# Splitting bn_stats passes over three slots, and a list scheduler that lets VectorE wait for a product

## The chip, the cores and the metric

One core of a Trainium2 chip. The metric is the device time of one execution in microseconds (us), lower is better. The kernel before had a median of 213.98 us in three runs (213.87 to 214.91).

The profiler's span is about 1.7 us shorter than the device time (212.9 us and 214.63 us for the profiled execution of before).

## The reference

```python
x = A_x                                   # (1, 2048, 512) bf16
xn = _layernorm(x)
# A: linear attention with softmax feature maps, 32 heads of 16
q, k, v = split(xn @ wqkv)
phi_q, phi_k = [softmax(+p), softmax(-p)] of q @ w_phi, k @ w_phi
o = (phi_q @ (phi_k^T v)) / (phi_q @ sum(phi_k) + 1e-6)
# B: gated bilinear unit, 1792 wide
h = (xn @ w_gate) * (xn @ w_up)
out = x + o @ wo + h @ w_down
```

## The kernel before

The kernel records steps (engine, function, tiles read and written) and a list scheduler orders them engine by engine. TensorE's order and the DMA queue's are pinned as recorded; those of VectorE, ScalarE and GpSimd follow from modelled costs. `prio` 0 is urgent, 1 normal, 2 filler. The parts that the change and the argument touch:

```python
def features(name, t, w, b=None):         # exponentials of +p and -p, their sums, logarithm, reciprocal
    ...
    dve(lambda e: e.tensor_reduce(out=sm, in_=e_v, axis=AX.X, op=ALU.add), ...)        # L506, "reduction"
    act(ln_v[:, n, :, sel], sm[:, :, sel], [("sums", sr)], [("ln", n)], func=ACTF.Ln)

def ln_apply(t):                           # L454, "normalisation"; xn has four slots
    ...
    dve(lambda e: e.tensor_scalar(out=xn_tile(t), in0=x_tile(t), ...), ..., [("xn", t % 4)] + ...)

def x_turn(t):                             # a transposing DMA from an xn slot: the slot is free when it has landed
    sc.dma(SP, lambda e: e.dma_start_transpose(o, xn_tile(t)), [("xn", t % 4)], [("xnT", t)], ..., turn=True)

def moments(chunks, after):                # sum of squares of the up weights, from bn_stats; L668
    sc.prio = 2
    for i in chunks:
        dve(lambda e, i=i: e.bn_stats(wst[:, i, :], wu_chunks[:, i, :]), keys + after, [("wst", i)], 512)
    ...

def gate(ft, sg, bg, bu, s):               # "product" of gate and up, L894: frees a bank (one of its output buffers) that TensorE needs
    act(g, bank(bg), ...)                  # the gate copy, ScalarE
    sc.prio = 0
    dve(lambda e: e.tensor_tensor(out=h_v[...], in0=bank(bu), in1=g, op=ALU.mult), ...)
    sc.prio = 1

def late_loads(t):
    ...
    elif t == 5:
        load_w(SP, wd_v, B_w_down..., "wd", 1835008)       # 1792 KB, ahead of the next transposes in the queue
        load_w(SP, wo_v, A_wo..., "wo", 524288)

def scales(t):
    ...
    if t in (5, 6):
        moments(range(7 * (t - 5), 7 * (t - 4)), last)

def _order(sc):
    ...
        soon = min(begin(p) for p in lst) + 100.0
        cand = min((p for p in lst if begin(p) <= soon), key=lambda p: (steps[p[1]].prio, begin(p), p[1]))
```

## Time and profile before

| | before, profiled execution |
|---|---|
| device time | 214.63 us (median of three runs 213.98) |
| span | 212.9 us |
| TensorE busy | 208.2 us, 98% |
| VectorE, ScalarE, GpSimd busy | 167.3, 143.8, 109.9 us |
| start of the first gate matmul (the first of 256 columns) | 9.07 us |
| from there to the end | 203.83 us |

Part 1 of the page of before (engine, busy us, share of the span, instructions) and the head of part 4, the chain of work that ended last:

```profile
PE 208.2 (98%) x1455; PEld 125.3 (59%) x1476; DVE 167.3 (79%) x281; ACT 143.8 (68%) x350; POOL 109.9 (52%) x137
...
PE 96%; DMA 1%; DVE 1%; issue 1%
```

TensorE bounds the kernel. How close it is to its limit cannot be judged by its busy share, because matmuls are pipelined, as the Trainium skill says ("Perfetto Trace Analysis", Identifying the Most-Contended Engine). This trace agrees: a matmul of 512 columns is drawn 379 ns long although the next one starts 216 ns after it, so a stall of up to 0.16 us leaves no idle time on TensorE. What shows the stalls is the distance from each matmul's start to the next. In this trace it is 216 ns for 512 columns, which agrees with the 215.7 ns of the skill ("TensorE: Matmul & The Clock Gate", Wait — 56ns, not 53.3ns?). After 10 us there are 21 steps one whole matmul too long. 1455 matmul records stand beside 1476 weight loads, so 21 records are missing; these steps are no stalls. Three others are: 0.133 us at 55.41, 0.143 us at 58.38 and 0.102 us at 60.24, together 0.38 us.

They show as idle times of the weight loads in the timeline of before (start us, us, engine, line, operation, tiles, shapes, count, and in brackets the idle time before and what ended it):

```profile
55.41 0.55 PEld L247 LDWEIGHTS ps<-arena 128*128 128x128 bf16 x4 [0.46 <-DVE arena L894]
...
58.37 0.55 PEld L247 LDWEIGHTS ps<-arena 128*128 128x128 bf16 x4 [0.47 <-DVE arena L894]
...
60.23 0.23 PEld L381 LDWEIGHTS ps<-arena 128*128 128x128 bf16 x4 [0.43 <-ACT arena L228]
```

The timeline of before, VectorE, leads to them (L454 normalisation, L894 product, L668 bn_stats, L506 reduction):

```profile
48.22 0.68 DVE L668 BATCH_NORM_STATS2 arena<-arena 128x6 f32<-128x512 bf16 x1
51.11 0.41 DVE L454 TENSOR_SCALAR arena<-arena 128x512 bf16<-128x512 bf16 x1 [2.20 <-DMA arena<-arena]
51.44 0.68 DVE L894 TENSOR_TENSOR arena<-ps,arena 128x512 bf16<-128x512 f32 x1
52.04 0.41 DVE L454 TENSOR_SCALAR arena<-arena 128x512 bf16<-128x512 bf16 x1
52.36 1.28 DVE L668 BATCH_NORM_STATS2 arena<-arena 128x6 f32<-128x512 bf16 x2
53.55 1.20 DVE L506 TENSOR_REDUCE arena<-arena 128x64 f32<-128x1024 bf16 x1
54.67 0.68 DVE L894 TENSOR_TENSOR arena<-ps,arena 128x512 bf16<-128x512 f32 x1
55.27 2.46 DVE L668 BATCH_NORM_STATS2 arena<-arena 128x6 f32<-128x512 bf16 x4
57.65 0.67 DVE L894 TENSOR_TENSOR arena<-ps,arena 128x512 bf16<-128x512 f32 x1
```

VectorE stands 2.20 us in front of a normalisation whose xn slot a transposing DMA still reads. A ready product, two bn_stats and the reduction queue behind it. ScalarE then waits for the reduction (timeline of before, ScalarE), and its gate copies are late in turn:

```profile
54.79 0.26 ACT L228 ACTIVATE arena<-arena 128x64 f32<-128x64 f32 x1 [3.17 <-DVE arena L506]
```

### The profile page before, as it was taken

The page shows a single profiled execution, that of the slowest core. Times are in us where ns is not written, and L with a number is a line of the kernel's source. Part 1 is how long each engine was busy: PE and PEld are TensorE (multiplying, and loading weights), DVE is VectorE, ACT ScalarE, POOL GpSimd, SP SyncE. Part 2 cuts the span into 40 slices and gives each one's busy share as a digit, 9 for nine tenths or more (in the row PEclk, how much of TensorE's full clock was granted, in tenths as well). Part 3 has the DMA queues.
Part 4 walks back from the last instruction along what each step waited for, and adds up shares of the span by engine and source line. Part 5 has one row for each costly group of instructions (what it writes and reads, how often), then busy time and mean ns, then how long its engine had stood idle before and what let it go on. Part 6 is the DMA issues. An engine that isn't in the chain of part 4 may idle for free.

```text
span 212.9 us, 4028 instructions
## 1 busy us (share of the span) xinstructions
PE 208.2 (98%) x1455; PEld 125.3 (59%) x1476; DVE 167.3 (79%) x281; ACT 143.8 (68%) x350; POOL 109.9 (52%) x137
## 2 busy tenths in 40 slices
PE   8999999999999999999999999999999999999995
PEld 3575444444444444444444444546888898899884
DVE  4687999985995656578699988996888898898622
ACT  5479899975789999987778977664544444432220
POOL 4031554540311355999995882004549559558540
PEclk9999999999999999999999999999999999999999
DMA  5999780899100030322721340413374646537611
GB/s 163 309 300 375 134 207 0 122 345 147 30 3 0 20 78 3 52 51 49 77 45 29 65 86 0 118 53 52 45 83 125 162 85 154 134 91 175 123 49 49
DMA packets 49251, 22.29 MB, mean 105 GB/s; under 512 B 38096, under 2 KB 47696, under 8 KB 49232
## 3 DMA queue, kind: packets, MB, share of 16 engines
q1 hardware_dynamic: 48272, 21.39, 46.0%
q10 hardware_dynamic: 960, 0.66, 1.0%
q8 instruction: 11, 0.18, 0.4%
q14 instruction: 8, 0.07, 0.2%
HBM read 11.03 MB, written 2.10 MB: 62 GB/s over the span
## 4 chain that ended last, share of the span: by engine, by line
PE 96%; DMA 1%; DVE 1%; issue 1%
PE ps L247 91%; PE ps L611 2%; PE ps L553 2%; DMA arena<-in_A_x_dram 1%; PE ps L381 1%; PE ps L474 1%; DVE arena L427 0%; DVE arena L924 0%; DVE arena L434 0%; PE ps L1001 0%
## 5 line engine op out<-in xcount | busy, mean ns | idle before, releaser
L247 PE MATMUL ps<-arena 128*128 128x512 bf16 (+2 forms) x1139 | 198.4, 329 | 1.1
L247 PEld LDWEIGHTS ps<-arena 128*128 128x128 bf16 (+1 forms) x1160 | 110.7, 98 | 73.8 <-ACT arena L228 1.2
L228 ACT ACTIVATE arena<-ps 128x512 bf16<-128x512 f32 (+3 forms) x117 | 58.6, 539 | 12.9 <-PE ps L247 7.0
L228 ACT ACTIVATE arena<-arena 128x32 f32<-128x32 f32 (+9 forms) x131 | 52.9, 423 | 11.3 <-DVE arena L506 7.2
L894 DVE TENSOR_TENSOR arena<-ps,arena 128x512 f16<-128x512 f32 (+1 forms) x56 | 38.2, 683 | 11.8 <-PE ps L247 6.1
L516 POOL TENSOR_TENSOR arena<-arena 128x1024 bf16<-128x1024 bf16 x16 | 31.8, 1995 | 26.8 <-ACT arena L228 26.8
L506 DVE TENSOR_REDUCE arena<-arena 128x64 f32<-128x1024 bf16 x32 | 38.2, 1210 | 7.6 <-ACT arena L228 7.5
L228 ACT ACTIVATE arena<-ps,arena 128x512 bf16<-128x512 f32 (+1 forms) x55 | 35.9, 672 | 10.9 <-PE ps L247 10.4
L855 POOL TENSOR_TENSOR arena<-arena 128x256 f16<-128x256 f16 x32 | 23.8, 755 | 14.3 <-DMA arena<-arena 13.2
L833 DVE TENSOR_TENSOR arena<-arena 128x896 f16<-128x896 f16 x32 | 26.0, 812 | 3.4 <-PE ps L247 3.4
L228 ACT ACTIVATE ps<-ps 128x256 f32<-128x256 f32 x24 | 8.8, 368 | 29.0 <-PE ps L247 27.0
L924 DVE SCALAR_TENSOR_TENSOR arena<-ps,arena 128x256 bf16<-128x256 f32 (+1 forms) x24 | 13.2, 565 | 8.9 <-PE ps L247 8.7
L773 POOL TENSOR_TENSOR arena<-arena 128x512 f16<-128x512 bf16 x14 | 16.3, 1175 | 5.7 <-DVE arena L894 5.2
L959 POOL TENSOR_TENSOR arena<-arena 128x512 f32<-128x512 f32 x8 | 9.5, 1190 | 17.0 <-ACT arena L228 17.0
L522 POOL TENSOR_TENSOR arena<-arena 128x512 bf16<-128x512 bf16 x16 | 17.0, 1060 | 0.8
L621 DVE TENSOR_TENSOR arena<-ps,arena 128x512 f16<-128x512 f32 x16 | 11.0, 686 | 1.3 <-ACT arena L228 0.5
L405 DVE BATCH_NORM_STATS2 arena<-arena 128x6 f32<-128x512 bf16 x16 | 10.4, 668 | 0.4 <-DMA arena<-in_A_x_dram 0.4
L520 POOL TENSOR_TENSOR arena<-arena 128x32 f32<-128x32 f32 x16 | 5.2, 326 | 10.4 <-ACT arena L228 5.8
L452 POOL TENSOR_SCALAR arena<-arena 128x1 f32<-128x1 f32 x12 | 3.2, 282 | 12.3 <-ACT arena L228 12.3
L668 DVE BATCH_NORM_STATS2 arena<-arena 128x6 f32<-128x512 bf16 x14 | 8.9, 680 | 0.0
L553 PEld LDWEIGHTS ps<-arena 128*128 128x128 bf16 x128 | 6.1, 97 | 3.5
L454 DVE TENSOR_SCALAR arena<-arena 128x512 bf16<-128x512 bf16 x12 | 5.4, 484 | 2.8 <-DMA arena<-arena 2.6
(54 smaller groups left out, 72.9 us busy)
## 6 DMA issues: line engine op xcount, KB each, us to landing
arena<-in_A_x_dram SPq DMA_DIRECT2D x8, 256.0 KB, 3.3
out_dram<-arena SPq DMA_DIRECT2D x15, 128.0 KB, 2.1
arena<-in_B_w_down_dram SPq DMA_DIRECT2D x1, 1792.0 KB, 10.1
arena<-in_A_x_dram SPq DMA_DIRECT2D x3, 512.0 KB, 4.4
arena<-arena SPq DMA_TRANSPOSE x44, 3.1
arena<-in_B_w_gate_dram SPq DMA_DIRECT2D x1, 640.0 KB, 8.7
arena<-in_B_w_up_dram SPq DMA_DIRECT2D x1, 640.0 KB, 9.9
arena<-in_B_w_gate_dram SPq DMA_DIRECT2D x1, 512.0 KB, 5.1
```

Source lines behind the costliest of these rows:

```text
L228: return sc.step(ACT, lambda e: e.activation(out=out_ap, in_=in_ap, func=func, scale=scale, **kw), reads, writes, 130.0 + 0.833 * n)
L247: ins = e.matmul(out_ap, lhsT=l, rhs=r, start=start and i == 0, stop=stop and i == npair - 1, **kw)
L405: dve(lambda e: e.bn_stats(stats_v[:, t, 0:6], x_tile(t)), [("x", t)], [("st", t)], 512)
L506: dve(lambda e: e.tensor_reduce(out=sm, in_=e_v, axis=AX.X, op=ALU.add), [(name, s, 0), (name, s, 1)], [("sums", sr)], 1024)
L516: pool(lambda e: e.tensor_tensor(out=e_w, in0=e_w, in1=r_w, op=ALU.mult), [(name, s, 0), (name, s, 1), ("rs", n)], [(name, s, 0), (name, s ...
L522: pool(lambda e: e.tensor_tensor(out=e_v[:, :, 1, :], in0=e_v[:, :, 1, :], in1=rat[:, :, None].to_broadcast([128, H, 16]), op=ALU.mult), [ ...
L621: dve(lambda e: e.tensor_tensor(out=o_tile(t).rearrange("p (b h f) -> p b h f", b=2, f=16), in0=nd[:, :, :, 0:16], in1=w_v[:, r].unsqueeze ...
L773: pool(lambda e, ft=ft: e.tensor_tensor(out=hH_v[:, ft, 0:512], in0=hT_v[:, ft, 0:512], in1=r2w, op=ALU.mult), [("hT", ft, 0), "r2w", ("x" ...
L833: dve(lambda e, k=k, i0=i0, i1=i1, op=op: e.tensor_tensor(out=s_block(p, k), in0=i0, in1=i1, op=op), ks + more, [s_key(p, k)] + over.get(k ...
L855: pool(lambda e, k=k, i0=i0, i1=i1, op=op: e.tensor_tensor(out=so_block(p, k), in0=i0, in1=i1, op=op), ks + [("so", p, m) for m in more], ...
L894: dve(lambda e: e.tensor_tensor(out=h_v[:, ft, sg * 512:(sg + 1) * 512], in0=bank(bu), in1=g, op=ALU.mult), [("ps", bu), ("g", s)] + ([("j ...
L924: dve(lambda e: e.scalar_tensor_tensor(out=o, in0=src, scalar=inv, in1=resid, op0=ALU.mult, op1=ALU.add), keys + [rkey, "inv"], [("ostg", ...
```

## The change

The intent: spread the 14 bn_stats as 5, 5 and 4 over three slots, and let an engine hold back from its next step, for up to a quarter of that step's modelled cost (or 100 ns, as before, if that is more), when an urgent step (such as a product) becomes ready in that time.

```diff
-        if t in (5, 6):
-            moments(range(7 * (t - 5), 7 * (t - 4)), last)
+        if 5 <= t < 8:
+            moments(range(5 * (t - 5), min(NF, 5 * (t - 4))), last)
...
-                soon = min(begin(p) for p in lst) + 100.0
-                cand = min((p for p in lst if begin(p) <= soon), key=lambda p: (steps[p[1]].prio, begin(p), p[1]))
+                head = min(lst, key=lambda p: (begin(p), steps[p[1]].prio, p[1]))
+                soon = begin(head) + max(100.0, 0.25 * costs[head[1]][0] if costs[head[1]] else 0.0)
+                cand = min((p for p in lst if begin(p) <= (soon if steps[p[1]].prio == 0 else begin(head) + 100.0)),
+                           key=lambda p: (steps[p[1]].prio, begin(p), p[1]))
```

What the two parts make of VectorE's queue around the late normalisation, read from the built programs:

```
before          normalisation, product, normalisation, 2 bn_stats, reduction, product, 4 bn_stats, product
5, 5, 4 alone   normalisation, product, normalisation, 1 bn_stats, reduction, product, 3 bn_stats, product
scheduler alone product, 2 normalisations, 2 bn_stats, reduction, product, 4 bn_stats, product
after           product, 2 normalisations, 1 bn_stats, reduction, product, 3 bn_stats, product
```

No instruction is added or removed, and up to about 45 us all engines' orders are the same.

## The prediction

> **What bounds the kernel.** TensorE: the page gives PE 208.2 us busy of a 212.9 us span (98%), and the chain of waits is 96% PE. Busy share does not tell what is left to win (the Trainium skill, "Perfetto Trace Analysis", Identifying the Most-Contended Engine, calls it a bad measure, since matmuls are pipelined), so I took the distance from each matmul's start to the next. The skill ("TensorE: Matmul & The Clock Gate", Wait — 56ns, not 53.3ns?) gives 215.7 ns at full clock for 512 columns; this trace agrees: almost every step is 216 ns. From 10 us on, some 22 steps are longer by exactly one matmul with nobody releasing them (missing records); only three are real stalls:
>
> - 55.41 us, +0.13, released by a product of gate and up on VectorE;
> - 58.38 us, +0.14, the same;
> - 60.24 us, +0.10, a weight fold, released by ScalarE.
>
> Together 0.38 us. The start (first real work at 4.5 us) and the tail after the last matmul are left alone, and TensorE's order is pinned. So 0.38 us (0.2%) is about all this change can win.
>
> **What it moves.** Nothing is removed or added: 14 bn_stats (680 ns each, 8.9 us) stay, as do products (680 ns) and reductions (1210 ns). The order on VectorE and ScalarE changes. The timeline before shows one cause behind all three stalls:
>
> - VectorE idles 2.2 us until 51.11, on a normalisation pass that waits for a transposing DMA. The product behind it (51.44 to 52.12) had its inputs near 48.8. Now it goes ahead of the pass, into the idle time.
> - Two bn_stats stand ahead of the feature reduction (53.55 to 54.76); now one. From these durations I estimate the reduction to start near 52.4, 1.1 us earlier.
> - ScalarE idles 3.17 us until 54.79 on that reduction, then runs packed to 61.16. Its queue, including the bank release at 60.19, comes about 1 us earlier: the +0.10 goes.
> - The product of 54.67 to 55.35 ends near 54.2: the first +0.13 goes.
> - Four bn_stats (2.46 us) before the product at 57.65 become three: it starts near 56.2, needed by 58.2: the +0.14 goes.
>
> **New costs.** bn_stats end some 1.5 us later than 63.0, and the small norms chain with them (cast at 65.0 before). The norms matmul stands near 70 us, and VectorE idles 0.7 and 1.7 us between: off the path. Before the output stage the masked sums end near 139.1 instead of 138.4, needed at 139.8. A bank has about 2.6 us from its last matmul to its next use, more than a reduction and a product: I expect no new stall over 0.1 us.
>
> **Prediction.** 213.98 - 0.38 = 213.6 us; 80% range 213.2 to 214.1 (three runs before spread from 213.87 to 214.91). Faster by over 2%: 0.01; within 2%: 0.98; slower by over 2%: 0.01.
>
> **What would show it.** Right: steps from 55 to 61 us are all 216 ns; ScalarE's idle before the feature logarithm shrinks from 3.17 to about 2 us; the product fills VectorE's gap near 49 us; span about 212.5; PE busy falls as much as the span. Wrong: a new PE wait released by VectorE or ScalarE, most likely between 56 and 76 us or 134 and 140 us.
>
> **What would make it wrong.** Three bn_stats still run together; if the real gate copy comes just after they began, a product is late and a stall comes back. Run-to-run spread may hide so small a gain.

## The result, and the profile after

| | before | after |
|---|---|---|
| median, first comparison (6 runs each) | 214.31 us | 214.89 us |
| range | 213.87 to 214.91 | 214.31 to 215.44 |
| ratio | | 1.0025, 95% interval 1.0001 to 1.0049 |
| profiled execution: span | 212.9 us | 213.7 us |
| first gate matmul at | 9.07 us | 10.31 us |
| from there to the end | 203.83 us | 203.40 us |
| stalls of TensorE in that part | 0.38 us | none |

A ratio is the mean time of one kernel's fast runs over that of the other's of the same rounds, so it is not quite the ratio of the medians.

The three stalls are gone from the trace, and the part after the first gate matmul is 0.43 us shorter. Yet the time rose. The lines of after that answer to those of before, VectorE's timeline first:

```profile
50.20 0.69 DVE L894 TENSOR_TENSOR arena<-ps,arena 128x512 bf16<-128x512 f32 x1
51.39 0.89 DVE L454 TENSOR_SCALAR arena<-arena 128x512 bf16<-128x512 bf16 x2 [0.50 <-DMA arena<-arena]
52.20 0.69 DVE L668 BATCH_NORM_STATS2 arena<-arena 128x6 f32<-128x512 bf16 x1
52.80 1.20 DVE L506 TENSOR_REDUCE arena<-arena 128x64 f32<-128x1024 bf16 x1
53.92 0.68 DVE L894 TENSOR_TENSOR arena<-ps,arena 128x512 bf16<-128x512 f32 x1
54.63 1.88 DVE L668 BATCH_NORM_STATS2 arena<-arena 128x6 f32<-128x512 bf16 x3
56.54 0.69 DVE L894 TENSOR_TENSOR arena<-ps,arena 128x512 bf16<-128x512 f32 x1
```

ScalarE's timeline of after: its idle time before the logarithm is 1.18 us instead of 3.17 us.

```profile
54.03 0.26 ACT L228 ACTIVATE arena<-arena 128x64 f32<-128x64 f32 x1 [1.18 <-DVE arena L506]
```

Part 1 and the head of part 4 of the page of after:

```profile
PE 209.1 (98%) x1476; PEld 125.4 (59%) x1476; DVE 167.3 (78%) x281; ACT 144.4 (68%) x350; POOL 109.8 (51%) x137
...
PE 95%; DMA 3%; DVE 0%; ACTq 0%; ACT 0%; issue 0%
```

A DMA has 3% of the chain now. The chain of after in its first microseconds (start us, us, what):

```profile
1.71 5.82 DMA arena<-in_A_wqkv_dram
7.53 0.14 issue
7.67 0.73 PE ps L247 x2
```

Two matmuls waited for a piece of the v weights, issued at 1.71 us and landed at 7.53 us. In the trace of before the same load, also issued at 1.71 us, landed at 5.85 us, and the chain of before does not go through it. The change touches no instruction there. So there are two questions: does the slower start belong to the change, and why did the removed stalls not show in the time?

### The profile page after: what moved, and what is told of

Its sections match the earlier page's. It is cut to its first block, busy times and chain, and to the rows that moved or that the text cites. A ratio compares the mean times of both kernels' runs of the same rounds, so it can differ in the third digit from the quotient of the medians.

```text
span 213.7 us, 4048 instructions
## 1 busy us (share of the span) xinstructions
PE 209.1 (98%) x1476; PEld 125.4 (59%) x1476; DVE 167.3 (78%) x281; ACT 144.4 (68%) x350; POOL 109.8 (51%) x137
## 4 chain that ended last, share of the span: by engine, by line
PE 95%; DMA 3%; DVE 0%; ACTq 0%; ACT 0%; issue 0%
PE ps L247 90%; DMA arena<-in_A_wqkv_dram 3%; PE ps L553 2%; PE ps L611 2%; PE ps L381 1%; PE ps L474 0%; DVE arena L924 0%; ACTq L292 0%; ACT L1195 0%
## 5 line engine op out<-in xcount | busy, mean ns | idle before, releaser
L553 PEld LDWEIGHTS ps<-arena 128*128 128x128 bf16 x128 | 6.1, 97 | 3.5
L611 PEld LDWEIGHTS ps<-arena 128*128 128x128 bf16 x128 | 6.2, 97 | 1.2
```

The source lines that it names most:

```text
L611: ins = e.matmul(bank(b0 + c // 4, (c % 4) * CW, CW), lhsT=ph[:, c, :], rhs=kvz_v[:, c, :], start=True, stop=True)
```

## The experiments

Theory A: the stalls exist only in executions in which the transposes land late; the change makes the kernel tolerant of that, and the start varies by itself. Theory B: the changed order costs time.

In the table, all times but the last column's are us after the start of the first gate matmul, so that the start is out of them. "Landing" is that of the first transpose behind the down weights, "reduction" the start of the first reduction after it. The last column is the device time (median, and range). Stalls are summed from the distances of matmul starts.

| trace | landing | reduction | stalls | to the end | device time |
|---|---|---|---|---|---|
| before (the page) | 41.94 | 44.48 | 0.38 | 203.83 | |
| before, again | 41.03 | 43.58 | 0 | 203.39 | 214.06 (213.94 to 214.81) |
| before, again, second | 40.81 | 43.35 | 0 | 203.40 | 214.03 (213.87 to 214.43) |
| after (the page) | 40.98 | 42.48 | 0 | 203.40 | 214.89 (214.31 to 215.44) |
| after, again | 40.24 | 42.09 | 0 | 203.40 | 214.12 (213.86 to 215.15) |
| after, again, second | 40.99 | 42.52 | 0 | 203.40 | 214.03 (213.80 to 214.15) |
| before, one more load | 41.73 | 44.27 | 0.18 | 203.58 | 214.59 (214.32 to 214.90) |
| after, one more load | 42.23 | 43.74 | 0 | 203.36 | 214.13 (213.85 to 214.42) |
| before, two more loads | 41.73 | 44.28 | 0.19 | 203.59 | 214.72 (214.26 to 215.22) |
| after, two more loads | 41.89 | 43.41 | 0 | 203.36 | 214.74 (213.94 to 215.14) |
| before, train | 39.88 | 42.42 | 0 | 203.39 | 222.44 (221.99 to 223.20) |
| after, train | 39.73 | 42.09 | 0 | 203.40 | 222.91 (222.46 to 223.29) |
| before, train, four loads | 42.11 | 44.65 | 0.54 | 203.96 | 222.87 (222.25 to 223.71) |
| after, train, four loads | 41.82 | 43.34 | 0 | 203.36 | 222.68 (221.88 to 223.13) |
| before, fixed start | 39.64 | 42.18 | 0 | 203.40 | 222.13 (221.85 to 222.32) |
| after, fixed start | 39.77 | 42.09 | 0 | 203.40 | 221.97 (221.85 to 222.29) |
| before, fixed start, six loads | 42.99 | 45.53 | 1.43 | 204.84 | 223.45 (223.21 to 223.81) |
| 5, 5, 4 alone, fixed start, six loads | 43.11 | 45.06 | 0.97 | 204.37 | 222.97 (222.80 to 223.13) |
| scheduler alone, fixed start, six loads | 44.05 | 46.14 | 2.02 | 205.42 | 223.05 (222.81 to 224.11) |
| after, fixed start, six loads | 43.16 | 44.68 | 0.60 | 203.99 | 222.48 (222.44 to 222.53) |

### 1. Both kernels again, unchanged

No edit: two copies of each, each its own load of the program, all on one chip.

> The kernel before, unchanged, as a null test. Theory A (the change removes the three stalls, 0.38 us, and the 0.9 us or so by which it measured slower lies wholly in the arrival of the first loads, which differs from one load of a program or one execution to the next): ratio to the kernel before off 1 by up to 0.003 although nothing differs; from the first gate matmul (first one of 256 columns) to the end 203.8 us with the same three stalls near 55 to 60 us. Theory B (the changed order itself costs time in a place that the stalls do not show): ratio 1.000 within 0.001.

> The changed kernel, unchanged. Theory A: no stall after 10 us; from the first gate matmul to the end 203.4 us, 0.4 us less than before; the time before that matmul anywhere from 9 to 10.5 us; the ratio anywhere from 0.997 to 1.003. Theory B: ratio again 1.0025 within 0.001.

> The kernel before once more, its own load of the program. Theory A: differs from the other copy of it by up to 0.3%, with the difference before the first gate matmul; 203.8 us after it. Theory B: within 0.1% of the other copy.

> The changed kernel once more. Theory A: 203.4 us from the first gate matmul to the end, ratio anywhere from 0.997 to 1.003. Theory B: 1.0025 within 0.001 of the kernel before.

Measured ratios to before: 0.9993 (0.9970 to 1.0017) and 0.9985 (0.9963 to 1.0006) for the two copies of before, 0.9996 (0.9969 to 1.0022) and 0.9981 (0.9960 to 1.0001) for the two of after. The 1.0025 did not come back. Theory A's expectation failed in one point that taught the most: I expected the three stalls in both copies of before, and there are none. The timeline of the first copy of before, VectorE:

```profile
50.00 0.41 DVE L454 TENSOR_SCALAR arena<-arena 128x512 bf16<-128x512 bf16 x1 [1.30 <-DMA arena<-arena]
50.33 0.68 DVE L894 TENSOR_TENSOR arena<-ps,arena 128x512 bf16<-128x512 f32 x1
50.93 0.40 DVE L454 TENSOR_SCALAR arena<-arena 128x512 bf16<-128x512 bf16 x1
51.25 1.28 DVE L668 BATCH_NORM_STATS2 arena<-arena 128x6 f32<-128x512 bf16 x2
52.45 1.20 DVE L506 TENSOR_REDUCE arena<-arena 128x64 f32<-128x1024 bf16 x1
```

It is the same queue in the same order, and four bn_stats follow here too. But the normalisation waited 1.30 us, not 2.20 us. The transposes stand in the DMA queue behind the 1792 KB of down weights, which took 10.1 us to land in the first trace and 9.0 us in this one. From part 6 of the two pages, before and its copy (KB each, median us from issue to landing):

```profile
arena<-in_B_w_down_dram SPq DMA_DIRECT2D x1, 1792.0 KB, 10.1
```

```profile
arena<-in_B_w_down_dram SPq DMA_DIRECT2D x1, 1792.0 KB, 9.0
```

### 2. The same, with the transposes later

One more load of 229 KB goes out right behind the down weights, or two (the second into device memory outside the core). It is emitted past the scheduler, so that every other instruction keeps its place:

```diff
             load_w(SP, wd_v, B_w_down..., "wd", 1835008)
+            pad_o = sb("pad", 0, 896)
+            pad_i = bass.AP(tensor=B_w_down.tensor, offset=B_w_down.offset, ap=[[896, 128], [1, 896]])
+            sc.steps[-1].extra = lambda e: e.dma_start(pad_o, pad_i)
...
                     ins.then_inc(dma_sems[st.lane[1]], 16)
+                    if st.extra is not None:
+                        st.extra(e).then_inc(dma_sems[-1], 16)
```

> The kernel before with one more load of 229 KB behind the down weights, so that the transposing DMAs behind it land about 1 us later (near 42.1 us after the first gate matmul instead of 40.8 to 41.0). All engines' orders are as before. Theory A (the three stalls are made by a late landing of these transposes, and the changed order tolerates a later one): stalls of 0.3 to 0.8 us in all between 40 and 55 us after the first gate matmul; 203.7 to 204.2 us from there to the end. Theory B (the three stalls were a chance of one execution, with another cause): no stalls, 203.4 us.

> The changed kernel with the same additional load. Theory A: no stall or under 0.1 us, 203.4 to 203.5 us from the first gate matmul to the end. Theory B: as the kernel before with this load.

> The kernel before with two more loads of 229 KB (the second into memory outside the core), landing near 43 us or later. Theory A: for every further us of lateness about 1 us more of stall: 1.2 to 2 us in all. Theory B: no stalls.

> The changed kernel with the same two loads. Theory A: stalls too, but 0.8 to 1.1 us less than the kernel before with them, the time by which its feature reduction stands nearer to the transposes. Theory B: as the kernel before with these loads.

A load cost 0.6 us, not 1 us, and in the runs with two loads the down weights themselves happened to land earlier (38.65 us after the first gate matmul, instead of 39.16 us with one load), so that two loads were no later than one. The expected stalls of before (0.3 to 0.8 us with one load, 1.2 us and more with two) and of after with two loads (some) failed for want of lateness. What the traces show answers the question all the same. With a landing at 41.73 us before stalls for 0.18 us; with one at 42.23 us, half a microsecond later, after does not stall. The waits of the weight loads, from 45 to 62 us, before with one more load and then after with it (line numbers are two higher here; us in total, times, longest):

```profile
PEld ps L249 <- DVE arena L896: 0.7, 2, 0.4
PEld ps L383 <- ACT arena L230: 0.4, 1, 0.4
PEld ps L249 <- ACT arena L230: 0.3, 1, 0.3
```

```profile
engine line waited for: us in total, times, longest us
```

The second view has a heading and nothing under it. Stalls this small cannot be read from the clock: the ratios to before were 1.0022, 1.0001, 1.0029 and 1.0035, and the trace of the fourth has no stall at all. The interval of the fourth, 1.0016 to 1.0055, leaves out 1. Its trace is of its fastest run (213.94 us), so what slowed the other three (214.53 to 215.14 us) is not shown.

### 3. A train of matmuls ahead of the start

To take the first loads out of the time, 40 constant matmuls go ahead of the first transpose on TensorE; and four more loads were added to two of the kernels.

```diff
     warm(1, 512, [("x", 0)])
+    hold_at = sc.steps[-1]
...
+    def train(e):
+        for _ in range(40):
+            ins = e.matmul(bank(7, 0, 512), ...)
+        return ins
+    hold_at.hold = train
```

> The kernel before with a train of 40 constant matmuls of 512 columns on TensorE ahead of its first transpose, so that all first loads have landed when it ends. Theory A (the run-to-run spread of 0.9 us and more is the arrival of the first loads): some 5 to 9 us longer (most of the train, less what the start no longer waits for), spread of the runs under 0.3 us, no stall. Theory B (the spread or the 1.0025 has another source): spread as before, 1 us.

> The changed kernel with the same train. Theory A: equal to the kernel before with the train within 0.1 us (no stalls in either), spread under 0.3 us. Theory B (the changed order costs 0.25%): 0.5 us longer than it.

> Train, and four more loads of 229 KB behind the down weights: the transposes land about 2.4 us later, 43.2 us after the first gate matmul if the rest stands as in the runs without the train. Theory A: 1 to 2 us of stalls in the trace, and 1 to 2 us longer than the kernel before with the train alone.

> The changed kernel with train and four loads. Theory A: 0.2 to 1 us of stalls, and 0.6 to 1.3 us faster than the kernel before with train and loads: here alone the change gains. Theory B: as the kernel before with train and loads, or 0.5 us slower.

This missed: the spread was 1.2 us, not under 0.3 us, and after with the train measured 0.47 us above before with it by the medians, as theory B had it. The traces tell why for the two executions that were profiled: they differ by 0.36 us, and so do their first gate matmuls. The matmuls of the train run at half rate (427 ns) until TensorE's clock rises, and that moment differs: by the records of the granted clock it came at 5.34, 6.09 and 3.51 us in the three runs of before, of after, and of before with four loads; the first gate matmul stands at 17.47, 17.83 and 16.57 us. Half of the difference in the one is the difference in the other, to within 0.03 us. The Trainium skill says that the window of the clock gate is free-running and that the moment at which the clock rises therefore varies by 500 ns either way ("TensorE: Matmul & The Clock Gate", What's actually happening); these traces agree that it varies, but by more: from 3.5 to 6.1 us, with the first matmul at 0.82 us in all three. So the train exchanged one lottery for another. Beyond the first gate matmul, both kernels with the train alone take 203.4 us with no stall; with four loads, before stalls for 0.54 us and after for none. Both are less than expected (1 to 2 us, and 0.2 to 1 us), because the transposes landed near 42 us and not at 43.2 us; by the medians after gains 0.19 us here, not 0.6 to 1.3 us.

### 4. A start that no lottery moves

TensorE's first transpose now waits for a chain of 20 constant writes on GpSimd, while a train of 36 constant matmuls runs on it. Two of the four kernels get six more loads.

```diff
+    def clock(e):                # on GpSimd, ahead of its first masked weight
+        for i in range(20):
+            ins = e.memset(hT_v[:, i % NF, (3 - i // NF) * 512:(4 - i // NF) * 512], 0.0)
+        ins.then_inc(go, 1)
...
+    after_hold.before = lambda e: e.wait_ge(go, 1)      # on TensorE, ahead of its first transpose
```

> The kernel before with its first transpose on TensorE held until a chain of 20 constant writes on GpSimd ends (some 13 to 14 us), while a train of 36 constant matmuls keeps TensorE's clock up. Neither the arrival of the first loads nor the moment at which the clock rises can now move the start (with the train alone, the two traces that differ by 0.9 us in their first gate matmul differ by 1.8 us in that moment). Theory A: spread of all runs under 0.4 us; rest after the first gate matmul 203.4 us.

> The changed kernel with the same fixed start. Theory A: within 0.1 us of the kernel before with it, spread under 0.4 us. Theory B (the changed order costs 0.25%): 0.5 us slower than it.

> Fixed start and six more loads of 229 KB behind the down weights (0.6 us each by the runs with one load): the transposes land near 43.3 us after the first gate matmul. Theory A: stalls of 1 to 2 us, and as much slower than the kernel before with the fixed start.

> The changed kernel, fixed start and the six loads. Theory A: its reduction stands 1.0 us nearer to the landing, so it stalls 0.8 to 1.2 us less than the kernel before with the same loads, and is 0.8 to 1.2 us faster than it by the clock (0.4 to 0.6%). Theory B: no faster.

The spread fell to 0.47 us, a little over the 0.4 us that I expected (in some executions the train, with a late clock, still ends after the writes: 17.08 instead of 16.72 us at the first gate matmul). The means of the runs are 222.07 us for before and 222.05 us for after: with the start fixed, neither a cost nor a gain of the change can be seen. The cost of 0.5 us that theory B asked for is not there; with five runs of each and a spread of 0.47 us, a difference of some 0.3 us could still hide (an estimate from the scatter of these ten runs).

With six more loads the ranges no longer touch: 223.21 to 223.81 us before, 222.44 to 222.53 us after, means 223.47 and 222.48, a gain of 0.99 us, of which the traces show 0.83 us as stalls. The timeline of before with fixed start and six loads, VectorE (line numbers are six higher):

```profile
59.81 0.41 DVE L460 TENSOR_SCALAR arena<-arena 128x512 bf16<-128x512 bf16 x1 [3.25 <-DMA arena<-arena]
60.14 0.69 DVE L900 TENSOR_TENSOR arena<-ps,arena 128x512 bf16<-128x512 f32 x1
60.74 0.41 DVE L460 TENSOR_SCALAR arena<-arena 128x512 bf16<-128x512 bf16 x1
61.06 1.28 DVE L674 BATCH_NORM_STATS2 arena<-arena 128x6 f32<-128x512 bf16 x2
62.26 1.20 DVE L512 TENSOR_REDUCE arena<-arena 128x64 f32<-128x1024 bf16 x1
```

The same of after with fixed start and six loads:

```profile
56.61 0.69 DVE L900 TENSOR_TENSOR arena<-ps,arena 128x512 bf16<-128x512 f32 x1
59.98 0.90 DVE L460 TENSOR_SCALAR arena<-arena 128x512 bf16<-128x512 bf16 x2 [2.68 <-DMA arena<-arena]
60.80 0.69 DVE L674 BATCH_NORM_STATS2 arena<-arena 128x6 f32<-128x512 bf16 x1
61.41 1.20 DVE L512 TENSOR_REDUCE arena<-arena 128x64 f32<-128x1024 bf16 x1
```

From the landing to the reduction before needs 2.54 us and after 1.52 us. TensorE's waits in the two, from 20 to 80 us, before and then after:

```profile
PE ps L251 <- DVE arena L900: 1.0, 1, 1.0
```

```profile
PE ps L251 <- DVE arena L900: 0.2, 1, 0.2
```

### 5. Each part alone, under the same lateness

The first kernel takes the split of the bn_stats alone, the second the scheduler's lines alone, both with the fixed start and six loads.

> Only the split of the bn_stats (5, 5 and 4 over three slots, old scheduler), fixed start and six more loads. Its queue on VectorE after the late transposes: normalisation, product, normalisation, one bn_stats, reduction. Against the kernel before one bn_stats (0.6 us of queue) less stands ahead of the reduction, so I expect 0.5 to 0.7 us less of stall than the 1.43 us of before: 0.7 to 0.9 us, 222.9 us by the clock.

> Only the scheduler's part (7 and 7 over two slots), fixed start and six more loads. Its queue: product ahead of both normalisations, then two bn_stats, reduction. The product's 0.6 us leaves the queue, but the second normalisation then waits for its own transpose, 0.5 us after the first, so I expect 0.3 to 0.5 us less of stall than before: 0.9 to 1.1 us, 223.1 us by the clock. If the two parts add up to the whole (0.83 us less), the sum holds; if either alone gives the whole, it does not.

The split alone stalls for 0.97 us against 1.43 us of before, a little outside the 0.7 to 0.9 us that I expected; by the clock 222.97 us. The scheduler alone measured 223.05 us, as expected, but its profile fell in the slowest of its executions (224.11 us), in which the transposes landed 1 us later than in the others; its 2.02 us of stalls may not be compared as they stand. What may be compared is the time from the landing to the reduction. In before it is 2.54 to 2.55 us with landings from 39.64 to 42.99 us, and in after 1.50 to 1.53 us with landings from 40.98 us on. (In the three traces of after with earlier landings the reduction stands at 42.09 us whatever the landing, and the timeline of each shows it waiting 0.26 or 0.27 us for ScalarE: there the transposes no longer hold it.) The table sets the kernels side by side:

| | landing to reduction |
|---|---|
| before (nine traces, 2.54 to 2.55) | 2.54 us |
| 5, 5, 4 alone | 1.95 us (0.59 less: one bn_stats of the queue) |
| scheduler alone | 2.09 us (0.45 less: a product out of the queue, less a wait for the second transpose) |
| after (the trace with fixed start and six loads) | 1.52 us (1.02 less) |

The two parts add up to the whole within 0.02 us, 0.59 + 0.45 = 1.04 us. And one line fits all six traces in which the product behind the reduction stalls TensorE, whatever the order: that stall is the start of the reduction less 44.35 us.

| trace | reduction | less 44.35 | stall seen |
|---|---|---|---|
| before (the page) | 44.48 | 0.13 | 0.13 |
| before, train, four loads | 44.65 | 0.30 | 0.30 |
| after, fixed start, six loads | 44.68 | 0.33 | 0.33 |
| 5, 5, 4 alone, six loads | 45.06 | 0.71 | 0.70 (0.05 at the product ahead of the reduction, 0.65 at the one behind it) |
| before, fixed start, six loads | 45.53 | 1.18 | 1.19 |
| scheduler alone, six loads | 46.14 | 1.79 | 1.79 |

The other two stalls, some 0.25 us together, follow behind it, and begin a little earlier (0.18 us with the reduction at 44.27 us).

## Why the prediction was wrong

Point by point:

- **TensorE bounds the kernel, and only three stalls are left to win.** Right for the trace that was read. Its sum, 0.38 us, is nearly what the traces differ by after the first gate matmul (0.43 us), but that agreement was luck. In the profiled execution of after the transposes landed at 40.98 us, and before with a landing at 41.03 us shows no stall either. That the change removes stalls is shown by the experiments with equal lateness, not by this first pair.
- **One cause behind all three: a normalisation waiting for a transpose, with product, bn_stats and reduction behind it.** Right. Lateness alone brings the stalls back (0.18, 0.19, 0.54 and 1.43 us), and the stall follows the reduction's start one for one.
- **The reduction comes about 1.1 us earlier, the product fills the idle gap, ScalarE's idle shrinks from 3.17 to about 2 us.** Right: it stands 1.02 us nearer to the landing. ScalarE's idle was 1.18 us, less than predicted, as the transposes also landed 0.96 us earlier in that execution; with that added it would be 2.14 us (an estimate).
- **No new stall.** Right: after shows none after the first gate matmul in any trace without more loads, and none with landings up to 42.23 us.
- **"213.98 - 0.38 = 213.6 us".** This step failed. The 0.38 us stood in one execution, of 214.63 us, in which the down weights took 10.1 us to land. It was subtracted from the median of runs, 213.98 us, although not every run has these stalls: the four other traces of before without more loads (two of them with the start altered) show none, with landings up to 41.03 us. The books balance without it: 214.63 less 0.43 us in the later part and 0.2 us at the start (first gate matmul at 9.07 instead of 8.87 us) is 214.0 us, the median. The change gains nothing in an execution that lands in time: with a fixed start the two kernels measured 222.07 and 222.05 us, and both take 203.40 us after the first gate matmul.
- **The range, 213.2 to 214.1 us.** Too narrow, and it missed: 214.89 us. The prediction left the start alone, as if it were constant; the first gate matmul stood 1.24 us later in the profiled execution of after than in that of before, three times the gain that was forecast. Runs of before alone spread from 213.83 to 215.69 us over all jobs (65 runs, its two copies not counted, mean 214.38 us); 18 runs of after have a mean of 214.36 us. The 1.0025 of the first six runs of after is not shown to be a cost of the change, and the record speaks against it: it did not recur in twelve more runs, and in the profiled one of the six the excess lies wholly ahead of the first gate matmul (1.24 us later, less the 0.43 us gained), where the change moves no instruction. The load of the v weights that was late there (7.53 us) landed at 5.59 and 5.71 us in the two copies of after, and at 6.32 and 6.52 us in before with the train, so its lateness does not follow the changed order. Why the loads land late in some executions, and why the first six runs of after were slower, stays open; only one of these six was traced.

"Run-to-run spread may hide so small a gain" stood in the text, but in an execution that lands in time there was no gain to hide. How often before lands late is not known: one of its three traces without any edit did. A mean gain of 0.1 or 0.2 us over all executions is therefore neither shown nor excluded by these runs. No version beats both kernels in these experiments: what remains above the stall-free 203.4 us is the start.

## What to carry to other kernels

Before a stall is subtracted from a median, see whether the profiled execution is itself a median one: here it was 0.65 us above it, and 0.38 us of that was the very stall. The wait behind a DMA was here a property of the execution as much as of the kernel (2.20 us in one, 1.30 us in the next); trace two or three executions, and then ask for the margin (landing to need) instead of the idle time, since a change of order that moves a margin gains only where the margin is used up. Here before first stalls with a landing somewhere between 41.03 and 41.73 us after the first gate matmul, and after between 42.23 and 43.16 us. Fixing the start cut the spread of the runs from 1.2 to 0.5 us, which was still too much to see an effect of 0.1%; what made the effect visible by the clock was to overdraw the suspected lateness until the ranges parted.

## What the Trainium skill lacked or had wrong

- "TensorE: Matmul & The Clock Gate": it has the run-to-run difference of the warm-up, but as 500 ns either way, which is less than these traces show, and not what it does to a measurement that puts constant matmuls first. Here the clock rose between 3.5 and 6.3 us after the span's start, and a train of 40 matmuls carried half of that into the time: spreads of 0.8 to 1.5 us, against 0.1 to 0.6 us where a chain on GpSimd fixed the start (but for the kernel with the scheduler's part alone, 1.3 us).
- "DMA: Bandwidth & Descriptors": it gives no run-to-run spread of a load. The same 1792 KB load of before took 10.1, 9.0 and 8.9 us in three executions without any change, and a 128 KB piece of weights issued at 1.71 to 1.73 us landed between 5.59 and 5.85 us in five traces of unchanged kernels and at 7.53 us in a sixth.
- "Perfetto Trace Analysis": it says that matmul busy time is a bad measure, but not that matmul records can be missing, nor how to tell one from a stall. Here 1455 matmuls stood beside 1476 weight loads; a missing record was a step longer by exactly one matmul (216 ns), in 20 of 21 cases with no releaser; the three stalls were of other lengths (0.10 to 0.14 us), and each had one.
